# Moving the wait for the last two stores from SyncE to GpSimd, and a barrier's gather ahead of it, at the end of a dense SiLU forward-and-backward kernel

## The chip, the cores and the metric

The kernel runs on one core of a Trainium2 chip. The metric is the device time of one execution in microseconds (us). A profiled execution also gives a trace: a record for every instruction and for every semaphore update. The "span" goes from the first to the last instruction of the program. Where the reported time begins and ends against these records is not shown, so only differences of it between runs are read here.

The change concerns the last 0.8 us of a 320 us program. So this document reads single semaphore waits, and it uses one number throughout: the **tail**, the time from the last increment of the last store's semaphore to the end of the span.

## The reference

```
h   = einsum("bsd,df->bsf", x, w1)        # B=1, S=2048, D=640, F=1536, bf16
out = einsum("bsf,fd->bsd", silu(h), w2)
return out, and the gradients of x, w1, w2 for a given grad_out
```

## The kernel before

The work is six groups of matmuls (two forward, two for the gradients of the hidden layer and of x, two for the weight gradients). ScalarE and VectorE copy the results from PSUM to SBUF, the two on-chip memories, and SyncE issues the DMAs that store them. The last weight-gradient block is stored in two pieces, so that the very last store is small (128 columns, 32 KB):

```
for k, (lo, hi) in enumerate(((0, FC - P), (FC - P, FC))):
    # ... 16 matmuls into gp[:, lo:hi], then a copy to g1[:, lo:hi] ...
    last_store = nc.sync.dma_start(out=gw1_v[:, dt_, fc*FC+lo : fc*FC+hi], in_=g1[:, lo:hi])
wait_for_last_store_last(nc, last_store.ins.name)
```

Behind the kernel's own instructions the framework places a closing block. All five engines go through two barriers, and between them GpSimd clears the program's semaphores (99 to 110). In the program order of each engine (read from the compiled program, shortened; "96" counts arrivals, "97" is the release; a gather is GpSimd's wait until the other four have arrived, and on the other four DRAIN is the instruction that carries an arrival, on SyncE also the last wait):

```
SyncE      wait 104,102 | wait 107,100 | wait 108,101 | wait 109,106 | wait 110,99 | drain: wait 105
           arrive (96+1) | wait for release (97) | arrive (96+1) | wait for release (97)
ACT,PE,DVE arrive        | wait for release      | arrive        | wait for release
GpSimd     drain | gather: wait 96>=4 | release 97+4 | reset drain | semaphore clear
           | second drain | second gather: wait 96>=4 | second release 97+4
```

Semaphore 104 belongs to the next-to-last store, 105 to the last one. A helper of the kernel before had already sorted SyncE's waits so that the last store is waited for last:

```
def wait_for_last_store_last(nc, name):
    # ... at finalization, of the closing block's first SyncE instruction:
    late = [w for w in waits if w.id in lanes]             # lanes: the last store's semaphore
    waits = late + [w for w in waits if w.id not in lanes] # the first of the list is waited for last
```

Somebody has to wait for the stores before the clear, since the clear resets the very semaphores that tell of them.

Of the kernel before, what the change touches and what calls it, by code (L numbers as in the profile page):

```python
# [39 lines left out]
    nc.at_finalize(move)  # L40


def wait_for_last_store_last(nc, name):



    def move(nc):
        blocks = nc.m.functions[0].blocks
        store = next(i for b in blocks for i in b.instructions if i.name == name)
        lanes = {u.id for u in store.sync_info.on_update}  # L50
        end = blocks[-1].instructions
        at = next(k for k, i in enumerate(end) if i.engine == mybir.EngineType.SP)
        waits = list(end[at].sync_info.on_wait)
        late = [w for w in waits if w.id in lanes]
        assert len(late) == 1 and not end[at].sync_info.on_update
        waits = late + [w for w in waits if w.id not in lanes]
        end[at] = copy.replace(end[at], sync_info=mybir.SyncInfo(on_wait=waits, on_update=[]))

    nc.at_finalize(move)

# [2 lines left out]
def kernel(  # L63
# [11 lines left out]
    nc = tc.nc  # L75
# [44 lines left out]
    def store_rows(c, pool):  # L120
        for scr, dst_v in ((oT_scr, out_v), (gxT_scr, gx_v)):
            o_sb = pool.tile([P, STC, D], dt_in, name="o_sb")
            nc.sync.dma_start_transpose(out=o_sb[:], in_=scr[:, c * SC:(c + 1) * SC])
            nc.sync.dma_start(out=dst_v[:, c * STC:(c + 1) * STC, :], in_=o_sb[:])
# [3 lines left out]
    def load_a_blk(fc, pool, tag=None):  # L128
        a_blk = pool.tile([P, ST, FC], dt_in, name="a_blk", tag=tag or "a_blk")
        nc.sync.dma_start_transpose(out=a_blk[:], in_=aT_scr[fc * FC:(fc + 1) * FC, :])  # L130
        a_blks.append(a_blk)
# [234 lines left out]
    with ExitStack() as fctx:  # L366
        ab2pool = fctx.enter_context(tc.tile_pool(name="ab2pool", bufs=NFC - 1))
        gbpool = fctx.enter_context(tc.tile_pool(name="gbpool", bufs=NFC))
        fpool = fctx.enter_context(tc.tile_pool(name="fpool", bufs=NFC))
        s1pool = fctx.enter_context(tc.tile_pool(name="s1pool", bufs=3))  # L370

        for fc in range(1, NFC):
            load_a_blk(fc, ab2pool)
        gh_blks = []
        for fc in range(NFC):
            gh_blk = gbpool.tile([P, ST, FC], dt_in, name="gh_blk")
            nc.sync.dma_start_transpose(out=gh_blk[:], in_=ghT_scr[fc * FC:(fc + 1) * FC, :])
            gh_blks.append(gh_blk)

        store_rows(NCH - 1, s1pool)  # L380

        gw2_v = gw2.rearrange("(ft p) d -> p ft d", p=P)
        g2T_v = g2T_scr[:].rearrange("(dt p) f -> p dt f", p=P)
        k = 0
        for fc in range(NFC):
            a_blk = a_blks[fc]
            g2T = fpool.tile([P, DT, FC], dt_in, name="g2T")
            for dt_ in range(DT):
                gp = ps_h.tile([P, FC], FP32, name="hp")
                for st in range(ST):  # L390
                    nc.tensor.matmul(  # L391
                        gp[:],
                        lhsT=go_nat[:, st, dt_ * P:(dt_ + 1) * P],
                        rhs=a_blk[:, st, :],
                        start=(st == 0),
                        stop=(st == ST - 1),
                    )
                if k % 2 == 0:
                    nc.scalar.activation(g2T[:, dt_, :], gp[:], ACT.Copy)  # L399
                else:  # L400
                    nc.vector.tensor_copy(out=g2T[:, dt_, :], in_=gp[:])  # L401
                k += 1
            nc.sync.dma_start(out=g2T_v[:, :, fc * FC:(fc + 1) * FC], in_=g2T[:])

        def store_gw2(fc):
            g2 = fpool.tile([P, FB, D], dt_in, name="g2")
            nc.sync.dma_start_transpose(out=g2[:], in_=g2T_scr[:, fc * FC:(fc + 1) * FC])
            nc.sync.dma_start(out=gw2_v[:, fc * FB:(fc + 1) * FB, :], in_=g2[:])

        gw1_v = gw1.rearrange("(dt p) f -> p dt f", p=P)  # L410
        k = 0
        for fc in range(NFC):
            gh_blk = gh_blks[fc]
            for dt_ in range(DT):
                if dt_ == DT // 2:
                    store_gw2(fc)
                if fc == NFC - 1 and dt_ == DT - 1:
                    for k, (lo, hi) in enumerate(((0, FC - P), (FC - P, FC))):
                        gp = ps_h.tile([P, FC], FP32, name="hp")
                        for st in range(ST):  # L420
                            nc.tensor.matmul(  # L421
                                gp[:, lo:hi],
                                lhsT=x_nat[:, st, dt_ * P:(dt_ + 1) * P],
                                rhs=gh_blk[:, st, lo:hi],
                                start=(st == 0),
                                stop=(st == ST - 1),
                            )
                        g1 = s1pool.tile([P, FC], dt_in, name="g1")
                        if k == 0:
                            nc.scalar.activation(g1[:, lo:hi], gp[:, lo:hi], ACT.Copy)  # L430
                        else:
                            nc.vector.tensor_copy(out=g1[:, lo:hi], in_=gp[:, lo:hi])  # L432
                        last_store = nc.sync.dma_start(
                            out=gw1_v[:, dt_, fc * FC + lo:fc * FC + hi], in_=g1[:, lo:hi]
                        )
                    wait_for_last_store_last(nc, last_store.ins.name)
                    continue
                gp = ps_h.tile([P, FC], FP32, name="hp")
                for st in range(ST):
                    nc.tensor.matmul(  # L440
                        gp[:],
                        lhsT=x_nat[:, st, dt_ * P:(dt_ + 1) * P],
                        rhs=gh_blk[:, st, :],
                        start=(st == 0),
                        stop=(st == ST - 1),
                    )
                g1 = s1pool.tile([P, FC], dt_in, name="g1")
                if k % 2 == 0:
                    nc.scalar.activation(g1[:], gp[:], ACT.Copy)
                else:  # L450
                    nc.vector.tensor_copy(out=g1[:], in_=gp[:])  # L451
                k += 1
                nc.sync.dma_start(out=gw1_v[:, dt_, fc * FC:(fc + 1) * FC], in_=g1[:])
# [30 lines left out]
```

## Time and profile before

The kernel took 320.86 us (median of 3 runs, 320.43 to 321.17).

From the page of the profile of before: the span, the busy time of each engine, and the chain of work that ended last.

```profile
span 318.9 us, 3632 instructions
...
PE 314.2 (99%) x1516; PEld 150.7 (47%) x1544; DVE 102.7 (32%) x182; ACT 76.8 (24%) x139; POOL 0.7 (0%) x6
...
PE 96%; DMA 2%; issue 1%; SPq 0%; DVE 0%; DVEq 0%
```

TensorE (PE) is the limit for all but the ends of the program; nothing that happens on another engine in the middle matters for this change. The next view cuts the end of the program into three stretches: up to the last matmul's result, up to the landing of the last store, and the tail. Columns: the stretch, its length, then each engine's busy time with its number of instructions, the granted clock, the DMA share and GB/s.

```profile
core 0: us, PE busy (x) PEld busy (x) DVE busy (x) ACT busy (x) POOL busy (x), PEclk, DMA share, GB/s
300.00:316.30 16.30, 16.23 (x91) 8.13 (x89) 1.38 (x2) 1.68 (x3) 0.00 (x0) 1.00 0.12 41
316.30:318.15 1.85, 0.00 (x0) 0.00 (x0) 0.29 (x1) 0.00 (x0) 0.00 (x0) 1.00 0.25 71
318.15:318.93 0.78, 0.00 (x0) 0.00 (x0) 0.00 (x0) 0.00 (x0) 0.00 (x0) 1.00 0.00 0
```

In the last 0.78 us nothing is busy: no engine computes and no DMA moves. That is barrier work, which this view does not count as busy. The waits of SyncE's queue (waiter, what it waited for, total us, times, longest) and the DMA issues (KB, us from issue to landing) name what leads up to it; L479 is the line under which all closing instructions are recorded.

```profile
SPq L479 <- DMA out_dram<-g: 0.8, 2, 0.6
SPq L479 <- PEq L479: 0.6, 2, 0.4
...
out_dram<-g SPq DMA_DIRECT2D x1, 96.0 KB, 1.6
out_dram<-g SPq DMA_DIRECT2D x1, 32.0 KB, 1.5
```

SyncE stood 0.8 us in its waits for the two stores. What then came behind the landing is shown by the view of line L479 for the stretch from the last increment to the end (engine and operation, count, duration in ns, first and last start). "q" is the engine's sequencer, PEldq is TensorE's.

```profile
L479 POOLq EVENT_SEMAPHORE  x4: 17/17/17, 318.3 to 318.8; - x4
L479 SPq DRAIN  x3: 7/7/13, 318.2 to 318.5; - x3
L479 SPq EVENT_SEMAPHORE  x2: 17/17/17, 318.4 to 318.9; - x2
L479 ACTq EVENT_SEMAPHORE  x2: 17/17/17, 318.4 to 318.9; - x2
L479 DVEq EVENT_SEMAPHORE  x2: 21/21/21, 318.4 to 318.9; - x2
L479 PEldq EVENT_SEMAPHORE  x2: 51/51/51, 318.4 to 318.9; - x2
L479 POOLq DRAIN  x2: 34/56/78, 318.4 to 318.7; - x2
L479 ACTq DRAIN  x1: 14/14/14, 318.5 to 318.5; - x1
L479 DVEq DRAIN  x1: 19/19/19, 318.5 to 318.5; - x1
L479 POOLq EVENT_SEMAPHORE_RANGE_CLEAR  x1: 96/96/96, 318.5 to 318.5; - x1
L479 PEldq DRAIN  x1: 13/13/13, 318.5 to 318.5; - x1
```

Nearly all of both barriers stands here, behind the store: two gathers and two releases on GpSimd (its four EVENT_SEMAPHOREs), two departures on each of the other four (their two EVENT_SEMAPHOREs), both of SyncE's arrivals, and the second arrival of ScalarE, VectorE and TensorE (one DRAIN each). Only the first arrivals of these three came earlier (314.9 to 316.4 us), so the first barrier waits for SyncE alone. The view rounds starts to 0.1 us. The records of the trace behind it give them exactly; starts in ns after the last increment of semaphore 105 (at 318.147 us):

```
SyncE   drain, waits for 105       17      GpSimd  semaphore clear       389
SyncE   arrives at first barrier   86      GpSimd  second drain          514
GpSimd  gather                    118      GpSimd  second gather         592
GpSimd  release                   197      GpSimd  second release        671
GpSimd  reset drain               282      TensorE last instruction      724, ends 775
```

### The profile page before, as it was taken

Reading aid. Unit: us, or ns where it says so; the run is one execution under the profiler, and the core shown is the slowest. Engines: PE = TensorE matmul, PEld = TensorE weight load, DVE = VectorE, ACT = ScalarE, POOL = GpSimd, SP = SyncE. Lnnn points to the kernel's source line nnn. Section 1 sums busy time; section 2 is a strip of 40 time slices with the busy share of each in tenths; the row PEclk is TensorE's granted clock in tenths of the full one; section 3 lists DMA queues with packets and bytes.
Section 4 is the critical chain, followed back from the end, with each engine's and each line's share of the span. In section 5 each row is a group of like instructions: output and inputs, shape, how many; then the busy total and the mean of one; then the engine's idle time right before and its main releaser. Section 6 shows DMA issues by size and latency. Waiting matters only on the chain.

```text
span 318.9 us, 3632 instructions
## 1 busy us (share of the span) xinstructions
PE 314.2 (99%) x1516; PEld 150.7 (47%) x1544; DVE 102.7 (32%) x182; ACT 76.8 (24%) x139; POOL 0.7 (0%) x6
## 2 busy tenths in 40 slices
PE   9999999999999999999999999999999999999996
PEld 7854444444444444444444444444444444444443
DVE  1494641477410187710147741000000100001001
ACT  2691000644201354311064420111100001001100
POOL 0000000000000000000000000000000000000000
PEclk9999999999999999999999999999999999999999
DMA  8999999999999866492544089919999999996111
GB/s 268 311 177 222 216 266 255 313 270 304 260 232 342 201 191 174 144 299 82 164 120 128 0 268 265 210 38 290 222 258 255 228 214 339 229 311 216 38 39 45
DMA packets 147233, 67.02 MB, mean 210 GB/s; under 512 B 113937, under 2 KB 146705, under 8 KB 147217
## 3 DMA queue, kind: packets, MB, share of 16 engines
q1 hardware_dynamic: 146928, 66.43, 83.0%
q10 hardware_dynamic: 288, 0.36, 0.3%
q8 instruction: 12, 0.20, 0.3%
q14 instruction: 5, 0.03, 0.0%
HBM read 9.18 MB, written 28.97 MB: 120 GB/s over the span
## 4 chain that ended last, share of the span: by engine, by line
PE 96%; DMA 2%; issue 1%; SPq 0%; DVE 0%; DVEq 0%
PE hp L302 32%; PE hp L286 16%; PE hp L391 16%; PE hp L440 15%; PE hp L204 12%; PE hp L233 3%; DMA w_nat<-in_w_dram 2%; PE hp L421 1%; SPq L173 0%; SPq L170 0%; DVE g L432 0%; DVEq L432 0%; SPq L468 0%
## 5 line engine op out<-in xcount | busy, mean ns | idle before, releaser
L286 PE MATMUL hp<-goT,w2T 128*128 128x512 bf16 x239 | 56.8, 379 | 0.1
L302 PE MATMUL hp<-ghT,w1T 128*128 128x512 bf16 x235 | 52.2, 379 | 0.3
L302 PE MATMUL hp<-aT,w_nat 128*128 128x512 bf16 x234 | 52.1, 379 | 0.3
L391 PE MATMUL hp<-a_blk,go_nat 128*128 128x512 bf16 x235 | 51.7, 379 | 0.3
L440 PE MATMUL hp<-gh_blk,x_nat 128*128 128x512 bf16 x219 | 48.2, 379 | 0.3
L204 PE MATMUL hp<-xT,w_nat 128*128 128x512 bf16 x174 | 43.4, 379 | 0.3
L310 ACT ACTIVATE oT<-hp 128x512 bf16<-128x512 f32 x24 | 14.5, 604 | 106.8 <-PE hp L302 106.8
L302 PEld LDWEIGHTS <-w1T 128*128 128x128 bf16 x240 | 23.5, 98 | 28.3
L391 PEld LDWEIGHTS <-go_nat 128*128 128x128 bf16 x240 | 23.5, 98 | 28.3
L286 PEld LDWEIGHTS <-w2T 128*128 128x128 bf16 x240 | 23.5, 98 | 28.3
L302 PEld LDWEIGHTS <-w_nat 128*128 128x128 bf16 x240 | 23.5, 98 | 28.1
L293 DVE SCALAR_TENSOR_TENSOR ghT<-ghT,hp 128x512 bf16<-128x512 bf16 x48 | 32.5, 681 | 7.3 <-PE hp L286 7.3
L440 PEld LDWEIGHTS <-x_nat 128*128 128x128 bf16 x224 | 21.9, 98 | 26.4
L312 DVE CAST oT<-hp 128x512 bf16<-128x512 f32 x16 | 11.1, 691 | 72.2 <-PE hp L302 67.7
L213 ACT ACTIVATE aT<-hp 128x512 bf16<-128x512 f32 x36 | 21.5, 597 | 30.4 <-PE hp L204 30.4
L204 PEld LDWEIGHTS <-w_nat 128*128 128x128 bf16 x180 | 17.6, 98 | 21.3
L220 DVE SCALAR_TENSOR_TENSOR ghT<-aT,v 128x512 bf16<-128x512 bf16 x36 | 24.6, 684 | 0.2
L219 DVE TENSOR_SCALAR v<-t 128x512 bf16<-128x512 f32 x36 | 15.4, 426 | 26.7 <-ACT t L217 26.7
L217 ACT ACTIVATE t<-hp 128x512 f32<-128x512 f32 x36 | 21.3, 592 | 0.0
L451 DVE CAST g<-hp 128x512 bf16<-128x512 f32 x7 | 4.8, 691 | 47.0 <-PE hp L440 34.5
L401 DVE CAST g2T<-hp 128x512 bf16<-128x512 f32 x7 | 4.8, 692 | 46.1 <-PE hp L391 46.1
L399 ACT ACTIVATE g2T<-hp 128x512 bf16<-128x512 f32 x8 | 4.8, 597 | 47.0 <-PE hp L391 47.0
(28 smaller groups left out, 77.3 us busy)
## 6 DMA issues: line engine op xcount, KB each, us to landing
aT_scr<-aT SPq DMA_DIRECT2D x4, 1536.0 KB, 6.3
ghT_scr<-ghT SPq DMA_DIRECT2D x4, 1536.0 KB, 8.2
out_dram<-o_sb SPq DMA_DIRECT2D x8, 640.0 KB, 3.3
oT_scr<-oT SPq DMA_DIRECT2D x4, 640.0 KB, 3.6
go_nat<-in_grad_out_dram SPq DMA_DIRECT2D x4, 640.0 KB, 8.3
gxT_scr<-oT SPq DMA_DIRECT2D x4, 640.0 KB, 4.7
w_nat<-in_w_dram SPq DMA_DIRECT2D x1, 1920.0 KB, 11.1
x_nat<-in_x_dram SPq DMA_DIRECT2D x3, 640.0 KB, 7.2
```

The source lines that it names most:

```text
L204: nc.tensor.matmul(hp[:], lhsT=w1_nat[:, dt_, ft * P:(ft + 1) * P], rhs=xT[:, dt_, :], start=(dt_ == 0), stop=(dt_ == DT - 1),)
L213: nc.scalar.activation(aT[:, ft, :], hp[:], ACT.Silu)
L217: nc.scalar.activation(t[:], hp[:], ACT.Tanh, scale=0.5)
L219: nc.vector.tensor_scalar(out=v[:], in0=t[:], scalar1=-0.5, scalar2=0.5, op0=ALU.mult, op1=ALU.add)
L220: nc.vector.scalar_tensor_tensor(out=ghT[:, ft, :], in0=aT[:, ft, :], scalar=1.0, in1=v[:], op0=ALU.subtract, op1=ALU.mult)
L286: nc.tensor.matmul(gp[:], lhsT=w2T[:, dt_, ft * P:(ft + 1) * P], rhs=goT[:, dt_, :], start=(dt_ == 0), stop=(dt_ == DT - 1),)
L293: nc.vector.scalar_tensor_tensor(out=ghT[:, ft, :], in0=ghT[:, ft, :], scalar=1.0, in1=gp[:], op0=ALU.add, op1=ALU.mult)
L302: nc.tensor.matmul(op_[:], lhsT=w_all[:, ft, dt_ * P:(dt_ + 1) * P], rhs=rhs_all[:, ft, :], start=(ft == 0), stop=(ft == FT - 1),)
L310: nc.scalar.activation(oT[:, dt_, :], op_[:], ACT.Copy)
L312: nc.vector.tensor_copy(out=oT[:, dt_, :], in_=op_[:])
L391: nc.tensor.matmul(gp[:], lhsT=go_nat[:, st, dt_ * P:(dt_ + 1) * P], rhs=a_blk[:, st, :], start=(st == 0), stop=(st == ST - 1),)
L440: nc.tensor.matmul(gp[:], lhsT=x_nat[:, st, dt_ * P:(dt_ + 1) * P], rhs=gh_blk[:, st, :], start=(st == 0), stop=(st == ST - 1),)
```

## The change

The intent: take both barriers' arrivals out of the chain behind the store. SyncE no longer waits for the last two stores and goes to the first barrier at once. GpSimd waits for them, on its reset drain. GpSimd's second gather moves ahead of that wait, so that the other engines' second arrivals, too, are collected while the store is still in flight. Behind the landing there should remain only reset drain, clear, second drain and second release. The core of the diff (cut):

```
-def wait_for_last_store_last(nc, name):
+def last_stores_end_on_pool(nc, names):
 ...
-        late = [w for w in waits if w.id in lanes]
-        waits = late + [w for w in waits if w.id not in lanes]
+        late = [w for lane in reversed(lanes) for w in waits if w.id == lane]
+        waits = [w for w in waits if w.id not in lanes]
         end[at] = copy.replace(end[at], sync_info=mybir.SyncInfo(on_wait=waits, on_update=[]))
+        pool = [i for i in end if i.engine == mybir.EngineType.Pool]
+        drain, gather, release, reset, clear, drain2, gather2, release2 = pool
+        closing = {i.name for i in (reset, clear, drain2, gather2)}
+        to = next(k for k, i in enumerate(end) if i.name == reset.name)
+        # ... the four are deleted from the block ...
+        reset = copy.replace(reset, sync_info=mybir.SyncInfo(on_wait=late, on_update=[]))
+        for i in (drain2, clear, reset, gather2):
+            end.insert(to, i)          # order on GpSimd: gather2, reset, clear, drain2
 ...
-                    wait_for_last_store_last(nc, last_store.ins.name)
+                        last_stores.append(store.ins.name)
+                    last_stores_end_on_pool(nc, last_stores)
```

The compiler splits the two waits on the reset drain: one wait instruction for 104, then the drain itself waits for 105.

More of the change, by code (lines that the diff above doesn't have):

```diff
@@ L40, in start_before_entry_wait @@
     nc.at_finalize(move)
-def wait_for_last_store_last(nc, name):
+def last_stores_end_on_pool(nc, names):
     def move(nc):
         blocks = nc.m.functions[0].blocks
-        store = next(i for b in blocks for i in b.instructions if i.name == name)
-        lanes = {u.id for u in store.sync_info.on_update}
+        stores = [next(i for b in blocks for i in b.instructions if i.name == name) for name in names]
+        lanes = [u.id for i in stores for u in i.sync_info.on_update]
         end = blocks[-1].instructions
@@ L53, in move @@
         waits = list(end[at].sync_info.on_wait)
-        late = [w for w in waits if w.id in lanes]
-        assert len(late) == 1 and not end[at].sync_info.on_update
-        waits = late + [w for w in waits if w.id not in lanes]
+        late = [w for lane in reversed(lanes) for w in waits if w.id == lane]
+        assert len(late) == len(names) and not end[at].sync_info.on_update
+        waits = [w for w in waits if w.id not in lanes]
         end[at] = copy.replace(end[at], sync_info=mybir.SyncInfo(on_wait=waits, on_update=[]))
+        pool = [i for i in end if i.engine == mybir.EngineType.Pool]
+        drain, gather, release, reset, clear, drain2, gather2, release2 = pool
+        assert gather2.sync_info.on_wait and not release2.sync_info.on_wait
+        assert all(i.sync_info is None or not i.sync_info.on_wait for i in (reset, clear, drain2))
+        closing = {i.name for i in (reset, clear, drain2, gather2)}
+        to = next(k for k, i in enumerate(end) if i.name == reset.name)
+        for k in reversed(range(len(end))):
+            if end[k].name in closing:
+                del end[k]
+        reset = copy.replace(reset, sync_info=mybir.SyncInfo(on_wait=late, on_update=[]))
+        for i in (drain2, clear, reset, gather2):
+            end.insert(to, i)
     nc.at_finalize(move)
@@ L417 @@
                 if fc == NFC - 1 and dt_ == DT - 1:
+                    last_stores = []
                     for k, (lo, hi) in enumerate(((0, FC - P), (FC - P, FC))):
@@ L432 @@
                             nc.vector.tensor_copy(out=g1[:, lo:hi], in_=gp[:, lo:hi])
-                        last_store = nc.sync.dma_start(
+                        store = nc.sync.dma_start(
                             out=gw1_v[:, dt_, fc * FC + lo:fc * FC + hi], in_=g1[:, lo:hi]
                         )
-                    wait_for_last_store_last(nc, last_store.ins.name)
+                        last_stores.append(store.ins.name)
+                    last_stores_end_on_pool(nc, last_stores)
                     continue
```

## The prediction

> **What bounds the kernel.** TensorE. The page gives PE 314.2 of 318.9 us busy, at a granted clock of 1.0, and the chain that ended last is 96% PE. The change touches only the tail after the last matmul, 316.3 to 318.9 us (the run reports 320.73, 1.8 beyond the span).
>
> **The tail before, from the trace's instruction and semaphore records (us).** The last cast ends at 316.67; SyncE issues the last store at 316.69 (0.33 long). The next-to-last store's 16 increments arrive from 317.38 to 317.58, the last store's from 317.97 to 318.15. SyncE's closing waits run from 317.59: the view of waits has SyncE's closing line waiting 0.8 us for the two stores. Its drain passes at 318.164, 17 ns after the last increment. Behind it stands a serial chain of starts:
>
> - SyncE arrives at the first barrier 318.233; GpSimd gathers 318.265, releases 318.344;
> - GpSimd's reset drain 318.429, semaphore range clear 318.536, second drain 318.661;
> - GpSimd gathers 318.739, releases 318.818; TensorE's last instruction runs 318.871 to 318.922.
>
> That is 0.76 us from wait passed to end of span.
>
> **What the change removes.** SyncE no longer waits for the two stores. It has about five other closing wait instructions, 65 ns apart in the trace, all satisfied; I estimate that it reaches the first barrier at about 317.40 instead of 318.23. The first gather, release, and the second barrier's arrivals (0.20 us from release to last arrival in the trace) are then done at about 317.75, and GpSimd has taken its second gather, while the last store is still in flight until 318.15. About 0.35 us of slack is left.
>
> **What stays serial behind the landing.** GpSimd's drain (with the wait for the last store), clear (+107 ns), second drain (+125), release (+78), then +53 and 51 ns to the end of TensorE's record: 318.17 + 0.41 = 318.58. Removed: 265 ns from SyncE's drain to GpSimd's reset drain, and the 79 ns from gather to release of the second barrier. Sum 0.34 us. Added: one more wait instruction on GpSimd (the earlier store, landed 0.57 us before), about 0.07 us, inside the slack, so free. GpSimd's wait may notice the landing slightly later than SyncE's did (its gather started 24 ns after the increment, against SyncE's 17): under 0.02 us. All of the 0.34 us lies on the critical path, and what follows the span should move along unchanged.
>
> The Trainium skill ("Perfetto Trace Analysis", section on sequencer-only instructions) says that a record holds only the execution, not the wait or the propagation of semaphores; this trace agrees (a 7 ns SyncE drain costs 32 ns until the next start), so I cost by start-to-start times.
>
> **Prediction.** 320.86 - 0.34 = 320.5 us, range 319.9 to 320.95, mostly run-to-run spread (before: 0.74 us over three runs). Faster by over 2%: 0.01; within 2%: 0.98; slower by over 2%: 0.01.
>
> **What would show it.** Right: span near 318.6; SyncE's closing waits for the two stores gone; SyncE's first barrier arrival near 317.4; GpSimd's reset drain starting within about 30 ns of the last increment; clear to end about 0.3 us. Wrong: GpSimd's drain starting over 0.1 us after the landing; the gather not yet taken when the store lands; the gap between span and reported time growing by what the span lost.
>
> **What would make it wrong.** A slow wake-up of GpSimd, a later landing of the store because barrier updates run beside its increments, or a longer stretch after the span.

## The result, and the profile after

After the change the kernel took 320.53 us (median of 6 runs, 320.35 to 320.94); the kernel before took 320.84 us in the 6 runs that stand beside them. The ratio is 0.9992, with a 95% interval from 0.9979 to 1.0004: within 2%, and not clear of noise. Ratios here are the mean time of one kernel's fast runs over that of the other's of the same rounds, so they are not quite the ratio of the medians quoted.

From the page of after, the span and the busy times:

```profile
span 318.8 us, 3632 instructions
...
PE 313.6 (98%) x1516; PEld 150.5 (47%) x1544; DVE 102.8 (32%) x182; ACT 76.8 (24%) x139; POOL 0.7 (0%) x6
```

The span alone would mislead: it fell by only 0.16 us in these two executions. The cut into stretches tells why; its bounds are again the last matmul's result and the landing of the last store.

```profile
300.00:316.48 16.48, 16.41 (x91) 8.22 (x90) 1.38 (x2) 1.69 (x3) 0.00 (x0) 1.00 0.12 41
316.48:318.34 1.86, 0.00 (x0) 0.00 (x0) 0.29 (x1) 0.00 (x0) 0.00 (x0) 1.00 0.25 71
318.34:318.77 0.43, 0.00 (x0) 0.00 (x0) 0.00 (x0) 0.00 (x0) 0.00 (x0) 1.00 0.00 0
```

In this execution the last matmul was 0.18 us later (316.48 instead of 316.30), because its start-up was 0.19 us longer (see e11). The middle stretch is the same, and the tail went from 0.78 to 0.43 us. SyncE's waits and the last two stores' times to landing, as shown of before:

```profile
SPq L494 <- PEq L494: 1.1, 2, 0.9
...
out_dram<-g SPq DMA_DIRECT2D x1, 96.0 KB, 1.6
out_dram<-g SPq DMA_DIRECT2D x1, 32.0 KB, 1.5
```

The wait for the two DMAs is gone from SyncE, the stores are as fast as before, and SyncE's idleness has moved to its waits for the barriers' releases, above all the second one (0.9 us; the view puts it down to TensorE's arrival, not to the store that GpSimd is waiting for). The closing line, L494 now, from the last increment to the end:

```profile
L494 POOLq DRAIN  x2: 34/56/78, 318.4 to 318.6; - x2
L494 POOLq EVENT_SEMAPHORE_RANGE_CLEAR  x1: 96/96/96, 318.5 to 318.5; - x1
L494 POOLq EVENT_SEMAPHORE  x1: 17/17/17, 318.7 to 318.7; - x1
L494 SPq EVENT_SEMAPHORE  x1: 17/17/17, 318.7 to 318.7; - x1
L494 ACTq EVENT_SEMAPHORE  x1: 17/17/17, 318.7 to 318.7; - x1
L494 DVEq EVENT_SEMAPHORE  x1: 21/21/21, 318.7 to 318.7; - x1
L494 PEldq EVENT_SEMAPHORE  x1: 51/51/51, 318.7 to 318.7; - x1
```

Of GpSimd's four gathers and releases one is left behind the landing, and the other engines have one departure each and no arrival. The same in ns after the last increment (at 318.337 us), from the records:

```
SyncE   arrives at first barrier -748      GpSimd  reset drain, waits for 105   25
GpSimd  gather                   -715      GpSimd  semaphore clear             131
GpSimd  release                  -637      GpSimd  second drain                256
GpSimd  second gather            -384      GpSimd  second release              320
GpSimd  wait for 104             -288      TensorE last instruction            374, ends 425
```

Everything in the left column is now hidden behind the store's 1.46 us from issue to landing.

### The profile page after: what moved, and what is told of

Read it like the earlier page. It is cut to its first block, busy times and chain, and to the rows that moved or that the text cites. A ratio compares the mean times of both kernels' runs of the same rounds, so it can differ in the third digit from the quotient of the medians.

```text
span 318.8 us, 3632 instructions
## 1 busy us (share of the span) xinstructions
PE 313.6 (98%) x1516; PEld 150.5 (47%) x1544; DVE 102.8 (32%) x182; ACT 76.8 (24%) x139; POOL 0.7 (0%) x6
## 4 chain that ended last, share of the span: by engine, by line
PE 96%; DMA 2%; issue 1%; SPq 0%; DVE 0%; DVEq 0%
PE hp L315 32%; PE hp L299 16%; PE hp L404 16%; PE hp L455 15%; PE hp L217 12%; PE hp L246 3%; DMA w_nat<-in_w_dram 2%; PE hp L435 1%; SPq L186 0%; SPq L183 0%; DVE g L446 0%; DVEq L446 0%; SPq L483 0%
```

## The experiments

Theory A is the one of the prediction: two pieces of a serial chain, 0.26 us (SyncE's arrival, first gather and first release) and about 0.08 us (second gather), moved behind the store, where there is slack for them. The rivals: B, the difference of the times is run-to-run drift, or the saved time comes back behind the span; C, the moved gather is what counts, or is worth its own time wherever the wait stands; D, GpSimd is slow to notice a wait; E, only the last store's wait needed to move; F, waits on GpSimd always cost.

Twelve experiments ran (ten different kernels with before and after; e0, e10, e11 and e9 repeat one of them), all with correct results. Diffs are against the changed kernel. All tails, with the reported time of the same profiled execution less the moment of the landing in it:

| run | tail us | reported less landing us |
|---|---|---|
| before, and e11 (before again) | 0.775, 0.775 | 2.583, 2.548 |
| after, e0, e10 (the change, three traces) | 0.425, 0.423, 0.424 | 2.203, 2.202, 2.207 |
| e1 wait moved, gather not | 0.517 | 2.298 |
| e2 gather moved, wait not | 0.965 | 2.737 |
| e3, e9 (clear waits, two traces) | 0.254, 0.254 | 2.065, 2.025 |
| e4 one store's wait moved, the other first on SyncE | 0.699 | 2.469 |
| e5 the same, the other last on SyncE | 0.424 | 2.214 |
| e6 nine more waits on GpSimd | 0.964 | 2.736 |
| e7 two more waits on GpSimd | 0.424 | 2.201 |
| e8 second release ahead of the wait | 0.146 | 1.979 |

### e0 and e10: the changed kernel, timed again

No edit.

> The changed kernel itself, timed in more rounds. Below, 'tail' is the time from the last increment of the last store's semaphore to the end of the span; it was 0.775 us in the trace of before and 0.425 us in that of after. Theory A (two pieces of serial chain hidden behind the store): tail 0.425 us within 0.02, and about 0.35 us less time than before. Rival B (the 0.31 us between the medians is run-to-run drift of the main part, and the shorter tail comes back in the stretch behind the span): the tail is short, but the times do not differ beyond noise and the reported time less the span grows by about 0.35 us.

> The changed kernel once more on the same chip and in the same rounds. Theory A: 0.35 us less than before, ratio about 0.9989, 0.17 us more than the version whose clear waits; tail 0.425 us. Rival B: no difference in the times.

Measured: e0 took 320.53 us (median of 6) against 321.01 (11 runs), ratio 0.9994 [0.9972, 1.0015]; e10 took 320.37 against 320.79 (11 runs), ratio 0.9984 [0.9965, 1.0003]. Each interval contains 1. Put together, the changed kernel's 18 runs have a mean of 320.63 us and the 28 runs of before beside them 320.97 us: 0.34 us less, with a standard error of 0.14 us (0.11 and 0.09 us for the two means). These runs come from more than one chip and are taken together without regard to it, so this is support and no more. The tails are the firm part: 0.423 to 0.425 us in three traces. Series by series the difference is 0.27, 0.16 and 0.54 us. The reported time counted from the landing is 2.20 or 2.21 us in all three and was 2.58 and 2.55 us in the two traces of before, so the stretch behind the span gave nothing back. The runtime's own records say the same: its last update of semaphore 2 (see e8) comes 2.71 and 2.68 us after the landing before, and 2.33 us in all three traces of the change. So the part of rival B by which the saved time comes back behind the span falls. The part by which the times do not differ is not refuted by the times of any one series; that the change saves time rests on the traces.

### e11: the kernel before, a second trace

No edit of the kernel before.

> The kernel before, unchanged, for a second trace. If the tail is a fixed sum of instruction times, it is 0.775 us within 0.01 again, with SyncE's drain 17 ns after the last increment, whatever the total time turns out to be. If the tail drifts from run to run as the total does, the differences of 0.1 to 0.5 us between tails shown so far rest on less than they seem to.

Measured: a tail of 0.775 us again, to the nanosecond of rounding, in an execution of 320.76 us. The three kernels that were traced more than once (before, the change, e3) repeat their tails within 2 ns; the total does not repeat like this.

Where the total's spread comes from shows in the same traces: the 61st weight load starts at 8.20 us in the quickest trace (e7) and at 10.62 us in the slowest (e8), and from there to the last weight load it is 307.493 or 307.494 us in thirteen of the fourteen traces (307.631 in e10). So most of the spread among these traces sits in the first 10 us of the program, while the first inputs arrive. What causes it there was not tried.

### e1: only the wait moves

```
-        for i in (drain2, clear, reset, gather2):
+        for i in (gather2, drain2, clear, reset):
```

> Only the first half of the change: GpSimd's reset drain waits for the two stores, but its second gather stays behind the semaphore clear, where before had it. Theory A: the first barrier is hidden, the second gather's 0.09 us is not; tail about 0.52 us (0.775 before, 0.425 after), time about 0.26 us under before. Rival C (the moved gather is what counts, since it hides the arrivals of four engines): tail near 0.75 us.

Measured: tail 0.517 us. GpSimd's closing instructions behind the landing at 318.262 us:

```profile
L494 POOLq DRAIN  x2: 34/56/78, 318.3 to 318.5; - x2
L494 POOLq EVENT_SEMAPHORE  x2: 17/17/17, 318.6 to 318.7; - x2
L494 POOLq EVENT_SEMAPHORE_RANGE_CLEAR  x1: 96/96/96, 318.4 to 318.4; - x1
```

By the records the reset drain starts 24 ns after the landing, the second gather 334 and the second release 412. So moving the wait is worth 0.258 us and moving the gather, once the wait has moved, 0.092 us. In time: 320.46 us against 321.01, ratio 0.9990 [0.9967, 1.0012].

### e2: only the gather moves

```
-        waits = [w for w in waits if w.id not in lanes]
+        waits = late + [w for w in waits if w.id not in lanes]
-        reset = copy.replace(reset, sync_info=mybir.SyncInfo(on_wait=late, on_update=[]))
```

> Only the second half of the change: the second gather stands ahead of the semaphore clear, but SyncE still waits for both stores ahead of the first barrier (last store last). Theory A: the gather has nothing to hide behind; the clear and the second drain, which in before ran while the four engines arrived at the second barrier, now wait for them, so the kernel gets slower: tail about 0.95 us (0.775 before). Rival C (moving the gather saves its own 0.09 us wherever the wait is): tail about 0.69 us.

Measured: tail 0.965 us, 0.19 us longer than before. From its closing line (L493 in this kernel), between the landing at 318.723 us and the end:

```profile
L493 POOLq EVENT_SEMAPHORE  x4: 17/17/17, 318.8 to 319.6; - x4
...
L493 PEldq DRAIN  x1: 13/13/13, 319.2 to 319.2; - x1
L493 POOLq EVENT_SEMAPHORE_RANGE_CLEAR  x1: 96/96/96, 319.4 to 319.4; - x1
```

The clear starts at 319.4, after TensorE's arrival at 319.2; in before the two were at 318.5 together. In before, GpSimd ran its reset drain and began its clear while the four engines arrived at the second barrier (TensorE last, at 399 ns), and so hid the arrivals. A gather in front of them serialises the two. So the same move costs 0.19 us without the other half and saves 0.09 us with it. About 0.03 us of the cost is TensorE's second arrival, which came 30 ns later in this trace (at 429 ns after the landing) than in before. From the first release to the second gather 253 or 254 ns pass in most traces with the gather moved, but 283 or 284 in e2, e8 and e10; the cause was not tried. In e8 and e10 the store hid it. Rival C, which expected 0.69 us, falls.

### e4 and e5: how many stores, and in what order

For e4 SyncE keeps the wait for 104, as its first; for e5, as its last.

```
e4: -        waits = [w for w in waits if w.id not in lanes]
    +        waits = [w for w in waits if w.id != lanes[-1]]
e5: +        waits = [late[1]] + [w for w in waits if w.id not in lanes]
both: on_wait=late -> on_wait=late[:1]       (on the reset drain)
```

> Only the last store's wait moves to GpSimd; SyncE keeps the wait for the next-to-last store, as the first of its closing waits. Theory A: SyncE passes it 0.55 us before the last store lands, then needs five more wait instructions of 65 ns and the two barrier steps, which end after the landing: tail about 0.70 us. Rival E (one moved wait is enough, the last store is the only one that matters): tail 0.425 us.

> As the run with one store's wait moved, but SyncE's wait for the next-to-last store is its last closing wait instead of its first. Theory A: SyncE arrives at the first barrier about 0.48 us before the last store lands, the second gather is taken about 0.12 us before it: tail 0.425 us as in after, with next to no slack. If the tail is 0.5 us or more, the barrier steps take longer than read from the trace.

Measured: 0.699 and 0.424 us. In e4, SyncE's queue waited for one store:

```profile
SPq L494 <- PEq L494: 0.7, 2, 0.6
SPq L494 <- DMA out_dram<-g: 0.6, 1, 0.6
```

By the records SyncE passed that wait 545 ns before the last landing, then needed five more wait instructions and reached the first barrier only 160 ns before the landing; the second gather came 204 ns after it. In e5, where those five were already done when 104 arrived, the tail is that of the change. So rival E is right only in e5's order. Which of the two engines waits for the next-to-last store does not matter as such; what matters is that the arrivals are over when the last store lands.

### e6 and e7: how much slack there is

e6 repeats nine waits that are long satisfied twice over on GpSimd's reset drain (ten wait instructions instead of one); e7 adds five of them (three instructions).

```
+        others = [w for w in waits if w.id not in lanes]
e6: on_wait=late -> on_wait=late + others + others
e7: on_wait=late -> on_wait=late + others[:5]
```

> The changed kernel with nine more wait instructions on GpSimd (ten instead of one) between the second gather and the reset drain, all on semaphores that have long been reached. Theory A (0.29 us of slack behind the store): at about 67 ns each the ten end 0.38 us after the landing, so the tail grows by about 0.36 us to 0.78 us, less than the 0.6 us that nine cost. Rival F (GpSimd's waits are on the critical path whatever the store does): the tail grows by all of 0.6 us, to about 1.0 us.

> The changed kernel with two more wait instructions on GpSimd (three instead of one, each for two semaphores long reached). In the trace of after, GpSimd's one wait instruction started 0.288 us before the last increment; in the run with ten such instructions a two-semaphore wait took 0.087 us until the next start. Theory A: three of them end 0.03 us before the landing, so the added 0.17 to 0.2 us is free: tail 0.425 us. Rival F (GpSimd's waits always cost): tail about 0.62 us.

Measured: e7's three waits are free (tail 0.424 us, the drain starts 24 ns after the landing). e6's tail is 0.964 us, longer than the 0.78 expected. GpSimd's closing instructions in e6, behind the landing at 318.764 us:

```profile
L495 POOLq EVENT_SEMAPHORE  x7: 17/43/43, 318.8 to 319.6; - x7
L495 POOLq DRAIN  x2: 34/56/78, 319.3 to 319.6; - x2
L495 POOLq EVENT_SEMAPHORE_RANGE_CLEAR  x1: 96/96/96, 319.4 to 319.4; - x1
```

Six of these seven are waits that ran out past the landing. A wait for two semaphores lasts 43 ns there, and 87 ns pass until the next start, where one on SyncE lasts 28 ns and takes 61 to 70; I had costed GpSimd's with SyncE's figure. With 87 the sum is right: the ten begin 281 ns before the landing and end 565 ns after it, 846 ns in all, of which the first is a single wait of 66 ns. Nine added instructions cost 780 ns on GpSimd, and 540 ns of that reached the tail. The rest, 0.24 us, is the slack. The trace of after says the same: the wait for 104 starts at -288 ns and takes 66, so the drain could have gone at -222 but went at +25, 0.247 us later. Rival F, for which all 780 ns would reach the tail (1.2 us), falls, and by e7 more plainly: e6's 0.964 us alone is nearer to the 1.0 us that was written down for rival F, with the wrong cost, than to theory A's 0.78.

### e3 and e9: the clear itself waits

```
-        reset = copy.replace(reset, sync_info=mybir.SyncInfo(on_wait=late, on_update=[]))
+        clear = copy.replace(clear, sync_info=mybir.SyncInfo(on_wait=late, on_update=[]))
-        for i in (drain2, clear, reset, gather2):
+        for i in (clear, drain2, reset, gather2):
```

> One step further than the change: GpSimd does both of its closing drains right behind the second gather, and the semaphore clear itself waits for the last store. Theory A: the 0.29 us of slack in the trace of after takes two more drains (about 0.1 us each), so 0.17 us more leaves the chain: tail about 0.255 us, time about 0.52 us under before. Rival D (a wait on the clear instruction is noticed late, or GpSimd's drains take longer there): tail 0.4 us or more.

> The version that went furthest without releasing the engines early, timed again, to see whether its 0.52 us (0.775 less 0.254 us of tail) comes out of the noise of the times. Theory A: 0.52 us less than before, ratio about 0.9984, tail 0.254 us again. Rival B: no difference in the times, or a tail that moves.

Measured: a tail of 0.254 us in both traces. From e3's closing line behind the landing:

```profile
L494 POOLq EVENT_SEMAPHORE_RANGE_CLEAR  x1: 96/96/96, 318.7 to 318.7; - x1
L494 POOLq EVENT_SEMAPHORE  x1: 17/17/17, 318.9 to 318.9; - x1
```

Both drains have moved into the slack; the clear starts 24 ns after the landing, as promptly as the drain did, so rival D falls. This version's tail is 0.17 us shorter than the change's and 0.52 us shorter than before. The times agree with it but do not show it: 320.09 us against 321.01 (ratio 0.9984 [0.9958, 1.0010]) and 320.41 against 320.79 (0.9987 [0.9960, 1.0014]), each with one run over 322 us among six. In its own rounds of the last series it was no faster than the change (320.41 against 320.37). In the traces it beats both kernels; in the times that is not settled.

### e8: the other engines leave before the store has landed

```
-        closing = {i.name for i in (reset, clear, drain2, gather2)}
+        closing = {i.name for i in (reset, clear, drain2, gather2, release2)}
-        reset = copy.replace(reset, ...)
+        clear = copy.replace(clear, sync_info=mybir.SyncInfo(on_wait=late, on_update=[]))
-        for i in (drain2, clear, reset, gather2):
+        for i in (clear, drain2, reset, release2, gather2):
```

> The extreme case: GpSimd releases the other four engines from the second barrier before it waits for the last store, and only GpSimd's clear is left behind the landing. Theory A for the span: it ends with the clear, tail about 0.12 us. For the reported time: if the stretch behind the span starts when the last engine is done, time about 0.65 us under before; if part of that stretch is work of the four other engines that can start early, more than 0.65 us. Rival B: the reported time does not fall below that of e3, the stretch behind the span grows instead.

Measured: tail 0.146 us; the clear is the only instruction behind the landing:

```profile
L494 POOLq EVENT_SEMAPHORE_RANGE_CLEAR  x1: 96/96/96, 320.3 to 320.3; - x1
```

It starts at +50 ns and not at +24, because the added release has used up the slack (the wait for 104 begins at -16 ns). But the reported time less the landing is 1.979 us, only 0.05 to 0.09 us under that of e3, although the span's tail fell by 0.108 us; the timed median is 320.30 against 321.01 (ratio 0.9985 [0.9963, 1.0008]). I had left two outcomes open for the reported time, 0.65 us under before or more. From the landing it is 0.57 to 0.60 us under before, so neither was met. Rival B, by which the stretch behind the span grows, is right in part: reported time less span is 1.83 us here, 1.77 and 1.81 in the two traces of e3's kernel. All this is one trace of e8, and two traces of one kernel differ by up to 0.04 us in this number.

The records behind the span tell why as far as they go. The Trainium skill ("Runtime: NRT & Kernel Launch", section on semaphores 0–2) names semaphore 2 as the runtime's "sync barrier", and the traces show it updated 18 times behind the span. In e8 the first two updates come 54 and 88 ns after the landing, presumably from engines that had left early (the records do not name them; the first comes 234 ns after TensorE's last instruction, 232 in after), and then nothing until 673 ns. In every other trace the third update comes 561 or 562 ns after GpSimd's last instruction has ended, and the second comes 0.18 to 0.21 us before the third. In e8 the second is 0.59 us ahead, and the third still comes 527 ns after GpSimd's end: it stayed with GpSimd when the others left. From the end of the clear, which is another instruction in the other kernels, the third update would be 764 ns in before, 671 in after, 608 in e3 and 527 in e8, so the clear is a worse match. The reading that fits is that the runtime's closing barrier is held up by GpSimd, and that the early departure of the four others buys nothing; it rests on the one trace in which GpSimd ends last. The small gain of e8 is that GpSimd itself ends 20 ns earlier (146 against 166 ns after the landing) and that its stretch is 35 ns shorter.

One caution on e8: it lets four engines go on before the semaphores are cleared. Here only the runtime's closing work follows. With another block of the program behind it, that would have to be thought through again.

## Why the prediction was right or wrong, point by point

- The time: 320.5 us predicted, 320.53 measured, inside the range. With a spread of 0.6 us among the six runs, the agreement of the medians to 0.03 us is luck; the mechanism is what is shown.
- "Sum 0.34 us": the tail fell by 0.350 us. The two terms were 265 ns for SyncE's arrival up to the first release and 79 ns for the second gather; e1 separates them as 258 and 92 ns. The second is larger because in the old place the second drain takes 78 ns until the gather and only 64 ns until the release.
- SyncE reaches the first barrier "at about 317.40": 317.589 in a trace whose last store was issued 0.186 us later, that is 317.403.
- "GpSimd has taken its second gather" about 0.40 us before the landing: 0.384 us. "0.35 us of slack is left" was too much: with the added wait paid, 0.247 us is left, since a gather takes 96 ns until the next instruction and the wait another 66.
- "Under 0.02 us" for a slower wake-up of GpSimd: 25 ns after the last increment against SyncE's 17, so 8 ns.
- "What follows the span should move along unchanged": confirmed; reported time less span was 1.77 to 1.81 us before and 1.78 us after. The prediction gave no reason. e8 suggests that the end that counts is GpSimd's, and the change moved that one along with the rest.
- "Span near 318.6" was not met in the profiled execution: 318.76 us, because its start-up was 0.19 us longer. The other signs were: first barrier arrival as above, GpSimd's reset drain 25 ns after the last increment, clear to end 0.29 us.
- "A later landing of the store" did not happen: from issue to last increment 1.455 us in both traces of before, 1.452 to 1.459 in the three of the change.
- What the prediction did not see: the halves of the change are not independent. It added 265 and 79 ns as if each stood alone; e2 shows that the second alone costs 0.19 us.

The Trainium skill ("Perfetto Trace Analysis", section on sequencer-only instructions) says that a record of such an instruction leaves out the semaphore wait and the propagation. The runs agree: GpSimd's second drain is recorded with 34 ns, but 64 or 78 ns pass until the next start. The recorded durations along the chain of before sum to 13+7+17+17+78+96+34+17+17+51 = 347 ns, of a tail of 775. Sums of start-to-start times met the tails of e0 to e8 within 0.02 us in seven of nine cases; e6 was off by 0.18 us (a spacing taken from the wrong engine) and e8 by 0.03 us (no slack left).

## What to carry to other kernels

Whatever must wait for the last store belongs as late in the closing sequence as correctness allows, and everything else, above all the arrivals of other engines, in front of it; but check what the moved step used to hide, because a gather put ahead of work that had covered it cost 0.19 us here. When an effect is a tenth of a percent and the runs spread by more, measure it from an event close by, here the store's landing (0.423 to 0.425 us in three traces), and treat the end-to-end time only as a check that nothing came back elsewhere. The engine that the runtime's closing work waits for need not be the one whose record ends the span: here, as far as e8's one trace shows, it was GpSimd, so its last instruction was the one to pull forward.

## What the Trainium skill lacked or had wrong

- "GPSIMD Engine Reference" has no cost of closing instructions on GpSimd. The runs show, from start to next start: a wait for one semaphore 66 ns, a wait for two mostly 87 ns (61 to 70 ns on SyncE), a reset drain 104 to 107 ns, the semaphore range clear 125 ns, a release to the next gather 253 to 284 ns when four engines have to arrive. GpSimd, when it stood waiting, went on 24 or 25 ns after the last increment, SyncE after 16 or 17 ns.
- "DMA: Bandwidth & Descriptors" splits the fixed time of a DMA (about 2.0 us; section on the anatomy of one DMA) for the path issued by GpSimd; for DMAs issued by SyncE it gives about 0.6 us to the first byte (section on latency and other measured facts) and no such split up to completion. Here the last store (32 KB to HBM, issued by SyncE) took 1.452 to 1.459 us from issue to last increment in all fourteen traces, and its first data packet started 0.83 us after the issue (counted from the start of the issuing record), so later than the page's figure; its last data packet ended 0.36 or 0.37 us before the last increment.
- The same page, on why a DMA increments by 16, says that each engine posts its increment as its data lands. The runs show sixteen single increments, not whose they are, and add the spread: the last store's came mostly 11 or 12 ns apart, 0.175 to 0.184 us from first to last.
- "Runtime: NRT & Kernel Launch", in its breakdown of the preamble and postamble, gives about 1.5 us for the closing barrier and 1.5 us for the semaphore reset. Here the first round of updates of semaphore 2 took 0.50 to 0.53 us (0.91 in e8), the reset 0.66 or 0.67 us, and the second round 0.36 us. That the first round is the whole of the page's closing barrier, and the updates of the other semaphores its reset, is assumed. The page does not say which engine holds the barrier up; here the third update came 561 or 562 ns after GpSimd's end in thirteen of fourteen traces.
